# The first two groups of a two-stage kernel run pair by pair, with loads issued in order of need and the first output stage on its own

## The chip, the core and the metric

The kernel runs on one core of one Trainium2 chip. The metric is the device time of one execution in microseconds (us), lower is better. The span of a profile is about 1.7 us shorter than the time of the same execution. Executions are sorted into fast and slow ones (slow: over 1.5% above the fastest of the same kernel); only fast ones are compared below unless the text says otherwise. In the views PE is TensorE (matmuls), PEld its weight loads, DVE VectorE, ACT ScalarE, POOL GpSimd and SP SyncE, which only issues transfers here. A *bank* is the piece of accumulator memory into which TensorE writes a result; an *eviction* is the copy out of it.

## The reference, cut to what matters

```python
for t in range(S):                       # per batch and head, gamma depends on the head
    state = gamma * state + outer(k[t], v[t])
    y[t] = scale * q[t] @ state
x = y, with heads joined                 # 3072 tokens x 512
h = x @ w_in                             # 512 -> 2048
out = (h * cos(h)) @ w_out               # 2048 -> 512
```

The kernel does the recurrence in chunks of 128 steps. One chunk of two batches is a *pair* (12 pairs); two pairs make a *group* of 512 token columns (6 groups). A pair is: conversion of q, k, v to bf16, stage T (transposes of q and k), stage A (scores), masks, stage Y (output into `xt`, and the state). A group then has 16 *F units* (x @ w_in for 128 features, then Sin and a multiply) and 16 *O units* (@ w_out).

## The kernel before

The loads of a pair are shared out between SP's queue and GpSimd's queue, and everything that GpSimd issues or converts stands in one program order:

```python
def load_pair(p):
    for t, src, engs in ((qf, q, (nc.sync, nc.sync)),
                         (kf, k, (nc.gpsimd, nc.gpsimd)),
                         (vf, v, (nc.sync, nc.gpsimd))):    # v of batch 0: SP
        for b in range(2): engs[b].dma_start(...)           # 256 KB each

def unit_f(g, f):                       # needs all 512 columns: both pairs of the group
    for i in range(KIN):
        nc.tensor.matmul(bank, lhsT=w_in_sb[:, i, ts(f, 128)], rhs=xt[g % 2][:, i, :], ...)
    cb = cosb[f % 3]
    nc.scalar.activation(out=cb, in_=bank, func=AF.Sin, bias=halfpi)
    nc.vector.tensor_tensor(out=gt[g % 2][:, f, :], in0=bank, in1=cb, op=ALU.mult)

# start (cut): pairs 0 and 1 without any F; GpSimd issues w_in, pairs 2 and 3, w_out, pair 4
for g in range(NG + 1):
    for s in range(16):
        hf, r = divmod(s, 8);  p = 2 * (g + 1) + hf
        if g < NG: unit_f(g, s)
        if g > 0:  unit_o(g - 1, *divmod(s, 4))
        if p < NP:
            if r == 0:   conv(p)            # q and v on GpSimd, k on VectorE
            elif r == 1: stage_t(p, False)
            elif r == 2: todo = stage_a(p); stage_m(p, todo[0])
            elif r == 3: stage_m(p, todo[1])
            elif r == 6: stage_y(p); ...    # and load_pair(p + 3)
```

## Time and profile before

| | before |
|---|---|
| time, median of 3 executions before the prediction (of 4 in the result) | 242.61 us (241.5) |
| span of the profiled execution | 239.4 us |
| first F unit, first O unit | 23.4 us, 57.8 us |
| first F unit of group 2 | 94.2 us |

This is the page's view of the span in 40 slices of 6 us. A digit is the busy share in tenths, PEclk is the granted TensorE clock. The row counts the time before the first clock record as full, which it was not: in this trace the record begins at about 26 us, and the F units at 23.36 and 25.02 us still take 0.42 us per 128x512 matmul, twice the later 0.216.

```profile
PE   0475409989699999999999999999999999999993
POOL 8907989259999706406024041000000000000000
PEclk9999956999889999999999999999999999999998
DMA  6999999999859354553071061101100111001212
```

From the twelfth slice on TensorE is full; nearly everything that is lost is lost before 66 us. There the DMA row is full and TensorE has holes. TensorE's waits (line, what it waited for, total, times, longest):

```profile
PE bank_67 L167 <- POOL qs_114 L145: 8.8, 1, 8.8
PE bank_69 L167 <- DVE qs_113 L145: 2.8, 1, 2.8
PE bank_63 L216 <- DVE am_1_1_131 L197: 2.2, 1, 2.2
PE bank_65 L167 <- DVE ks_116 L158: 1.2, 1, 1.2
```

The longest, 8.8 us, is for pair 2's q as converted by GpSimd. Busy time by stretch (stretch and its length, then the busy time of PE, PEld, DVE, ACT and POOL, granted clock, DMA share, GB/s); the last row is a group in the steady part:

```profile
25.20:37.00 11.80, 3.01 (x20) 1.71 (x18) 2.14 (x4) 1.93 (x3) 11.07 (x13) 0.68 1.16 267
57.00:93.60 36.60, 34.60 (x271) 17.03 (x270) 21.76 (x32) 18.79 (x28) 26.94 (x29) 0.95 0.71 189
93.60:127.00 33.40, 33.40 (x276) 17.01 (x275) 19.72 (x32) 19.51 (x29) 11.56 (x13) 1.00 0.39 103
```

TensorE works 3.0 of 11.8 us from 25 to 37 us while GpSimd (the fifth number) is busy for 11.1. A steady group takes 33.4 us. The chain of work that ended last (start, length, what) says what GpSimd was busy with:

```profile
6.34 13.21 DMA vf_0_100<-in_v_dram
19.63 2.04 POOL vs_119 L150 x2
23.31 6.85 DMA kf_1_93<-in_k_dram
34.24 1.09 POOL qs_114 L145
60.48 2.86 DVE ks_116 L158 x2
```

One tile, pair 1's v of batch 0 on SP's queue, took 13.2 us to land; GpSimd stood waiting for it, issued the rest of w_in and the loads of pairs 2, 3, w_out and pair 4 after it, and only then converted pair 2's q.

### The profile page before, as it was taken

How to read it: one execution, taken by the hardware profiler on the slowest of the kernel's cores; microseconds unless marked ns; L12 is line 12 of the kernel's file. 1: busy time of each engine (PE TensorE's matmuls, PEld its weight loads, DVE VectorE, ACT ScalarE, POOL GpSimd, SP SyncE). 2: the span in 40 equal slices, each digit the busy share in tenths (PEclk: the TensorE clock that was granted, in tenths of full speed). 3: DMA queues.
4: the chain of work that ended last, by engine and by line, in shares of the span. 5: the costliest groups of instructions: out<-in, count | busy, mean ns of one | idle time of the engine just before them, and what ended most of it. 6: DMA issues, size and time to landing. Idle time of an engine off the chain costs nothing.

```text
span 239.4 us, 4178 instructions
## 1 busy us (share of the span) xinstructions
PE 210.8 (88%) x1664; PEld 108.1 (45%) x1664; DVE 122.0 (51%) x203; ACT 118.8 (50%) x174; POOL 84.0 (35%) x96
## 2 busy tenths in 40 slices
PE   0475409989699999999999999999999999999993
PEld 0264105545345545545555455455455454444441
DVE  4565213968674473466556654753855624343100
ACT  2542305776435655556645646556465564544210
POOL 8907989259999706406024041000000000000000
PEclk9999956999889999999999999999999999999998
DMA  6999999999859354553071061101100111001212
GB/s 164 328 201 222 272 261 196 253 276 297 215 164 267 101 164 98 154 151 92 0 178 44 21 157 45 48 1 47 44 31 16 44 47 44 6 38 44 90 44 88
DMA packets 48020, 29.63 MB, mean 124 GB/s; under 512 B 38529, under 2 KB 42625, under 8 KB 48001
## 3 DMA queue, kind: packets, MB, share of 16 engines
q1 hardware_dynamic: 40896, 15.73, 25.7%
q0 software_dynamic: 7104, 13.63, 22.9%
q8 instruction: 13, 0.21, 0.3%
q14 instruction: 7, 0.05, 0.1%
HBM read 27.26 MB, written 6.29 MB: 140 GB/s over the span
## 4 chain that ended last, share of the span: by engine, by line
PE 74%; DMA 8%; DVE 7%; POOL 3%; issue 2%; SPq 2%; ACT 1%; DVEq 0%; ACTq 0%
PE bank_66 L254 14%; PE bank_63 L254 7%; PE bank_69 L240 6%; PE bank_65 L240 6%; DMA vf_0_100<-in_v_dram 6%; PE bank_64 L240 5%; PE bank_67 L240 5%; PE bank_68 L240 5%; PE bank_67 L254 4%; PE bank_63 L240 4%; PE bank_69 L254 3%; PE bank_68 L254 3%; DMA kf_1_93<-in_k_dram 3%; DVE gt_136 L244 3%; SPq L107 2%
## 5 line engine op out<-in xcount | busy, mean ns | idle before, releaser
L240 PEld LDWEIGHTS <-w_in_sb 128*128 128x128 bf16 x384 | 36.1, 99 | 41.4 <-issue 3.0
L254 PEld LDWEIGHTS <-gt_136 128*128 128x128 bf16 x192 | 19.0, 99 | 23.3 <-issue 1.1
L254 PEld LDWEIGHTS <-gt_137 128*128 128x128 bf16 x192 | 18.8, 98 | 22.7
L254 PE MATMUL bank_66<-w_out_sb,gt_136 128*128 128x512 bf16 x96 | 24.6, 379 | 0.0
L243 ACT ACTIVATE cosb_138<-bank_65,halfpi 128x512 bf16<-128x512 f32 x14 | 9.6, 687 | 15.9 <-PE bank_65 L240 15.9
L254 PE MATMUL bank_63<-w_out_sb,gt_136 128*128 128x512 bf16 x64 | 17.3, 395 | 0.0
L254 PE MATMUL bank_66<-w_out_sb,gt_137 128*128 128x512 bf16 x64 | 16.4, 379 | 0.0
L240 PE MATMUL bank_69<-xt_135,w_in_sb 128*128 128x512 bf16 x44 | 12.1, 402 | 0.0
L254 PE MATMUL bank_67<-w_out_sb,gt_137 128*128 128x512 bf16 x48 | 11.8, 380 | 0.0
L243 ACT ACTIVATE cosb_140<-bank_64,halfpi 128x512 bf16<-128x512 f32 x9 | 6.2, 687 | 9.7 <-PE bank_64 L240 9.7
L240 PE MATMUL bank_63<-xt_134,w_in_sb 128*128 128x512 bf16 x40 | 10.3, 380 | 0.0
L233 DVE CAST stb_133<-st_ps 64x512 bf16<-64x512 f32 x12 | 8.3, 688 | 3.3 <-PE st_ps L228 3.1
L240 PE MATMUL bank_65<-xt_134,w_in_sb 128*128 128x512 bf16 x32 | 9.1, 411 | 0.3 <-ACT xt_134 L220 0.3
L240 PE MATMUL bank_64<-xt_135,w_in_sb 128*128 128x512 bf16 x36 | 9.3, 380 | 0.0
L240 PE MATMUL bank_65<-xt_135,w_in_sb 128*128 128x512 bf16 x36 | 9.3, 380 | 0.0
L240 PE MATMUL bank_67<-xt_135,w_in_sb 128*128 128x512 bf16 x36 | 9.3, 380 | 0.0
L167 PE MATMUL bank_67<-ident,qs_114 128*128 128x128 bf16 x8 | 1.0, 263 | 8.8 <-POOL qs_114 L145 8.8
L240 PE MATMUL bank_68<-xt_134,w_in_sb 128*128 128x512 bf16 x32 | 8.2, 380 | 0.0
L240 PE MATMUL bank_64<-xt_134,w_in_sb 128*128 128x512 bf16 x32 | 8.2, 380 | 0.0
L240 PE MATMUL bank_68<-xt_135,w_in_sb 128*128 128x512 bf16 x32 | 8.2, 379 | 0.0
L254 PE MATMUL bank_68<-w_out_sb,gt_136 128*128 128x512 bf16 x32 | 8.2, 379 | 0.0
L254 PE MATMUL bank_69<-w_out_sb,gt_137 128*128 128x512 bf16 x32 | 8.2, 380 | 0.0
(361 smaller groups left out, 474.5 us busy)
## 6 DMA issues: line engine op xcount, KB each, us to landing
w_in_sb<-in_moe_w_in_dram POOLq DMA_DIRECT2D x4, 512.0 KB, 8.7
w_out_sb<-in_moe_w_out_dram POOLq DMA_DIRECT2D x4, 512.0 KB, 12.6
out_dram<-ob_108 SPq DMA_DIRECT2D x6, 256.0 KB, 2.1
out_dram<-ob_109 SPq DMA_DIRECT2D x6, 256.0 KB, 2.0
out_dram<-ob_110 SPq DMA_DIRECT2D x6, 256.0 KB, 2.0
out_dram<-ob_111 SPq DMA_DIRECT2D x6, 256.0 KB, 2.0
qf_0_78<-in_q_dram SPq DMA_DIRECT2D x3, 256.0 KB, 4.1
qf_1_79<-in_q_dram SPq DMA_DIRECT2D x3, 256.0 KB, 4.7
```

What stands on the lines that cost most here:

```text
L107: engs[b].dma_start(out=t[p % PRE][b], in_=src[2 * bp + b, :, ds(c * C, C)].rearrange("h t d -> t h d"))
L167: nc.tensor.transpose(tr[:, w, a, :], src[:, b, 2 * a : 2 * a + 2, :], ident)
L233: nc.vector.tensor_copy(out=stb[(p + 1) % 2][ts(j, 64), :, :, ts(j, 64)], in_=st_ps[ts(j, 64)])
L240: nc.tensor.matmul(bank, lhsT=w_in_sb[:, i, ts(f, 128)], rhs=xt[g % 2][:, i, :], start=(i == 0), stop=(i == KIN - 1))
L243: nc.scalar.activation(out=cb, in_=bank, func=AF.Sin, bias=halfpi)
L244: nc.vector.tensor_tensor(out=gt[g % 2][:, f, :], in0=bank, in1=cb, op=ALU.mult)
L254: nc.tensor.matmul(bank, lhsT=gt[g % 2][:, f, ts(j, 128)], rhs=w_out_sb[:, f, :], start=(f == 0), stop=(f == KOUT - 1))
```

## The change

The intent: let F start as soon as one pair is there, have F of group 1 to do while the data of pairs 2 and 3 come, and issue loads in the order in which they are needed. The core of the diff (cut):

```diff
-    def load_pair(p): ...
+    def load(eng, p, names): ...              # any tile on any queue
+    def pair_f(p, r):                         # F on the 256 columns of one pair
+        g, hf = divmod(p, 2)
+        for f in (4 * r, 4 * r + 2):
+            bank = banks.take()
+            for e in range(2):                # two f tiles to a bank
+                for i in range(KIN):
+                    nc.tensor.matmul(bank[:, ts(e, 256)], lhsT=w_in_sb[:, i, ts(f + e, 128)],
+                                     rhs=xt[g % 2][:, i, ts(hf, 256)], ...)
+            act(bank, gt[g % 2][:, f : f + 2, ts(hf, 256)])
...
+    load(nc.gpsimd, 1, ("k0", "k1", "v0", "v1"))     # v0 of pairs 1 to 3 no longer on SP
+    load_w_in(0); load_w_in(1)
+    for p in (2, 3): load(nc.sync, p, ("q0", "q1"))
+    load(nc.sync, 4, ("q0", "q1", "v0"))
+    conv_v(0, nc.gpsimd); conv_v(1, nc.gpsimd)
+    load(nc.gpsimd, 2, ("k0", "k1", "v0", "v1"))
+    load_w_in(2); load_w_in(3)
+    load(nc.gpsimd, 3, ("k0", "k1", "v0", "v1"))
+    conv_v(2, nc.gpsimd)
+    for r in range(4): load_w_out(r)
+    load(nc.gpsimd, 4, ("k0", "k1", "v1"))
...
+    stage_t(1, True);  pair_f(0, 0);  m1 = stage_a(1); masks(1, m1);  pair_f(0, 1)
+    stage_y(1, nc.scalar.copy)
+    conv_q(2, nc.vector); conv_k(2, True)            # were GpSimd and VectorE
+    pair_f(1, 0); pair_f(1, 1);  stage_t(2, False);  pair_f(0, 2);  ...   # to pair_f(3, 3)
-    for g in range(NG + 1):
+    for g in range(1, NG + 1):                       # g == 1: O(0) with pairs 4, 5, no F
-            if g < NG: unit_f(g, s)
+            if 1 < g < NG: unit_f(g, s)
```

The semicolons join lines of the original. In the loop a pair's conversions also move from its own first slot to the fifth slot of the pair before.

More of the change, by code (lines that the diff above doesn't have):

```diff
@@ L98, with load @@
     gk = sb([128, NC, H], FP32, "gk")
-    def load_pair(p):
+    SRC = {"q": (qf, q), "k": (kf, k), "v": (vf, v)}
+    def load(eng, p, names):
         bp, c = divmod(p, NC)
-        for t, src, engs in ((qf, q, (nc.sync, nc.sync)),
-                             (kf, k, (nc.gpsimd, nc.gpsimd)),
-                             (vf, v, (nc.sync, nc.gpsimd))):
-            for b in range(2):
-                engs[b].dma_start(
-                    out=t[p % PRE][b],
-                    in_=src[2 * bp + b, :, ds(c * C, C)].rearrange("h t d -> t h d"))
+        for n in names:
+            t, src = SRC[n[0]]
+            b = int(n[1])
+            eng.dma_start(
+                out=t[p % PRE][b],
+                in_=src[2 * bp + b, :, ds(c * C, C)].rearrange("h t d -> t h d"))
     def load_w_in(r):
@@ L123 @@
                    allow_small_or_imprecise_dtypes=True)
-    load_pair(0)
+    load(nc.sync, 0, ("q0", "q1", "v0"))
+    load(nc.sync, 1, ("q0", "q1"))
+    load(nc.gpsimd, 0, ("k0", "k1", "v1"))
     make_identity(nc, ident)
@@ L200, in stage_m, with stage_y @@
             banks.give(bk[j])
-    def stage_y(p):
+    def stage_y(p, copy_st=nc.vector.tensor_copy):
         c = p % NC
@@ L232, in stage_y, with act @@
         for j in range(2):
-            nc.vector.tensor_copy(out=stb[(p + 1) % 2][ts(j, 64), :, :, ts(j, 64)],
-                                  in_=st_ps[ts(j, 64)])
+            copy_st(out=stb[(p + 1) % 2][ts(j, 64), :, :, ts(j, 64)], in_=st_ps[ts(j, 64)])
+    f_no = [0]
+    def act(bank, out):
+        cb = cosb[f_no[0] % 3]
+        f_no[0] += 1
+        nc.scalar.activation(out=cb, in_=bank, func=AF.Sin, bias=halfpi)
+        if len(out.shape) == 3:
+            cb = cb.rearrange("p (f t) -> p f t", f=2)
+            bank = bank.rearrange("p (f t) -> p f t", f=2)
+        nc.vector.tensor_tensor(out=out, in0=bank, in1=cb, op=ALU.mult)
     def unit_f(g, f):
@@ L241, in unit_f @@
                              start=(i == 0), stop=(i == KIN - 1))
-        cb = cosb[f % 3]
-        nc.scalar.activation(out=cb, in_=bank, func=AF.Sin, bias=halfpi)
-        nc.vector.tensor_tensor(out=gt[g % 2][:, f, :], in0=bank, in1=cb, op=ALU.mult)
+        act(bank, gt[g % 2][:, f, :])
         banks.give(bank)
+    def pair_f(p, r):
[5 more added lines that the diff above has]
+                    nc.tensor.matmul(bank[:, ts(e, 256)], lhsT=w_in_sb[:, i, ts(f + e, 128)],
+                                     rhs=xt[g % 2][:, i, ts(hf, 256)],
+                                     start=(i == 0 and e == 0), stop=(i == KIN - 1),
+                                     skip_group_check=True)
+            act(bank, gt[g % 2][:, f : f + 2, ts(hf, 256)])
+            banks.give(bank)
     o_bank = {}
@@ L261, in unit_o, with masks @@
             nc.sync.dma_start(out=out[ds((2 * bp + j % 2) * S + c * C, C), :], in_=o)
-    load_pair(1)
+    load(nc.gpsimd, 1, ("k0", "k1", "v0", "v1"))
     load_w_in(0)
+    load_w_in(1)
+    for p in (2, 3):
+        load(nc.sync, p, ("q0", "q1"))
+    load(nc.sync, 4, ("q0", "q1", "v0"))
+    conv_v(0, nc.gpsimd)
+    conv_v(1, nc.gpsimd)
+    load(nc.gpsimd, 2, ("k0", "k1", "v0", "v1"))
+    load_w_in(2)
+    load_w_in(3)
+    load(nc.gpsimd, 3, ("k0", "k1", "v0", "v1"))
+    conv_v(2, nc.gpsimd)
+    for r in range(4):
+        load_w_out(r)
+    load(nc.gpsimd, 4, ("k0", "k1", "v1"))
+    def masks(p, items):
+        for it in items:
+            stage_m(p, it)
     conv_q(0, nc.vector)
     conv_k(0, True)
-    conv_v(0, nc.gpsimd)
     stage_t(0, True)
-    load_w_in(1)
-    load_w_in(2)
     m0 = stage_a(0)
-    for it in m0:
-        stage_m(0, it)
+    masks(0, m0)
+    conv_k(1, True)
     conv_q(1, nc.vector)
-    conv_k(1, True)
-    conv_v(1, nc.gpsimd)
-    load_w_in(3)
+    stage_y(0, nc.scalar.copy)
     stage_t(1, True)
-    stage_y(0)
+    pair_f(0, 0)
     m1 = stage_a(1)
-    for it in m1:
-        stage_m(1, it)
-    load_pair(2)
-    load_pair(3)
-    stage_y(1)
-    for r in range(4):
-        load_w_out(r)
-    load_pair(4)
-    def conv(p):
-        conv_q(p, nc.gpsimd)
-        conv_k(p, False)
-        conv_v(p, nc.gpsimd)
+    masks(1, m1)
+    pair_f(0, 1)
+    stage_y(1, nc.scalar.copy)
+    conv_q(2, nc.vector)
+    conv_k(2, True)
+    pair_f(1, 0)
+    pair_f(1, 1)
+    stage_t(2, False)
+    pair_f(0, 2)
+    m2 = stage_a(2)
+    masks(2, m2)
+    pair_f(1, 2)
+    pair_f(0, 3)
+    stage_y(2)
+    pair_f(1, 3)
+    conv_v(3, nc.gpsimd)
+    conv_q(3, nc.gpsimd)
+    load(nc.sync, 5, ("q0", "q1", "v0"))
+    load(nc.gpsimd, 5, ("k0", "k1", "v1"))
+    conv_k(3, False)
+    pair_f(2, 0)
+    pair_f(2, 1)
+    stage_t(3, False)
+    pair_f(2, 2)
+    m3 = stage_a(3)
+    masks(3, m3)
+    pair_f(2, 3)
+    stage_y(3)
+    conv_q(4, nc.vector)
+    conv_k(4, False)
+    conv_v(4, nc.gpsimd)
+    load(nc.sync, 6, ("q0", "q1", "v0"))
+    load(nc.gpsimd, 6, ("k0", "k1", "v1"))
+    for r in range(4):
+        pair_f(3, r)
     todo = []
-    for g in range(NG + 1):
+    for g in range(1, NG + 1):
         for s in range(16):
@@ L300 @@
             p = 2 * (g + 1) + hf
-            if g < NG:
+            if 1 < g < NG:
                 unit_f(g, s)
-            if g > 0:
-                unit_o(g - 1, *divmod(s, 4))
+            unit_o(g - 1, *divmod(s, 4))
             if p < NP:
-                if r == 0:
-                    conv(p)
-                elif r == 1:
+                if r == 1:
                     stage_t(p, False)
@@ L314 @@
                     stage_m(p, todo[1])
+                elif r == 4 and p + 1 < NP:
+                    conv_q(p + 1, nc.gpsimd)
+                    conv_k(p + 1, False)
+                    conv_v(p + 1, nc.gpsimd)
                 elif r == 6:
@@ L317 @@
                     if p + 3 < NP:
-                        load_pair(p + 3)
+                        load(nc.sync, p + 3, ("q0", "q1", "v0"))
+                        load(nc.gpsimd, p + 3, ("k0", "k1", "v1"))
 _INS = ['q', 'k', 'v', 'moe_w_in', 'moe_w_out']
```

## The prediction

> **What bounds the kernel now.** From 66 us TensorE hardly waits: in 100.9–134.0, 134.0–167.4 and 167.4–201.0 us the busy-time table shows it busy throughout at granted clock 1.00. There an F or O unit (four 128x512 matmuls) takes 0.863 us, and a group of 16 F, 16 O and two pairs 33.4 us, so 2.9 us per pair. An estimate of all TensorE work is 192 x 0.863 + 12 x 2.9 = 200 us; with 4.9 us before the first matmul and 3.9 us after the last, 209 us. The span is 239.4 us: about 30 us are lost, all in the start.
>
> The chain of waits and TensorE's waits show where: 8.8 us for qs_114 (pair 2), which GpSimd converts only at 34.2 us, although its q landed at 24.1 us: it first issues pairs 2 to 4 and w_out. 2.8 + 2.2 us for pair 1's conversions and masks; vf_0_100 lands 13.2 us after its issue. TensorE runs cold to about 39 us: 0.42 us per 128x512 matmul at 25 us against 0.216 later (granted clock 0.50 in 30–36 us), the state which the Trainium skill, "TensorE: Matmul & The Clock Gate", Part 1, describes for an idle array.
>
> DMA is nearly full up to 60 us (about 250 GB/s). SP's queue moves 256-byte packets and starves beside GpSimd's large ones (40,896 packets for 15.7 MB against 7,104 for 13.6 MB); the Trainium skill, "DMA: Bandwidth & Descriptors", Queues, rings and completion order, says that the engines alternate by packet. SP's 8th, 10th and 12th tiles landed at 24, 35 and 50 us.
>
> **What the change does.** No arithmetic is removed. 256 half-length matmuls are added in place of 128 full ones (estimate 0.11 us each), two f tiles to a bank, so Sin and multiply stay 0.69 us per bank. Weight loads should stay hidden: a load plus a 128-column transpose already takes only 0.055 us. F can start on one pair; F of group 1 fills the waits for pairs 2 and 3; pair 2's q conversion moves to VectorE.
>
> Estimate by engine order: w_in quarter 0 lands and F(0) starts about 17 us (before: 23.4); TensorE is nearly solid from 27 us; pair 2 transposes at 31 us (before: 35.4); pair 3's q (SP's ninth tile) lands about 30–35 us and is converted by 40 us. F of both groups and pairs 0–3 end at about 62 us. Then O(0) alone with pairs 4 and 5: 13.8 + 5.8 us plus about 3 us of new waits, since one 0.86-us unit separates transposes from stage A while two 1.0-us evictions lie between. Group 2 begins at 84.5 us, before at 100.9: 16.4 us earlier. The rest is unchanged.
>
> **Prediction: 226 us, 8 in 10 between 220 and 233.** Faster by over 2%: 0.94; within 2%: 0.05; slower: 0.01.
>
> **Right or wrong will show in:** the first F matmul near 17 us; full clock from about 25 us with 128x256 matmuls 0.11 us apart; no wait over 3 us after 27 us; O(0) from 62 us with waits on qkt evictions; group 2 at 84 us; 33.4 us per group after it.
>
> **What would make it wrong:** N=256 matmuls limited by weight loads (over 0.13 us: +5 us or more); SP's q tiles of pairs 2 and 3 later than 24 and 35 us; multiplies ahead of pair 2's masks stalling TensorE until it goes cold; or fewer stalls than I count, giving 215–220 us.

## The result

The changed kernel took 225.78 us (median of 4 fast executions, 225.59 to 225.99) against 241.5 us (239.88 to 242.84). The ratio is 0.9352, 95% interval 0.9279 to 0.9425. Here and below a ratio is the mean time of one kernel's fast runs over that of the other's of the same rounds, so not quite the ratio of the medians.

| | before | after |
|---|---|---|
| first F unit | 23.4 us | 16.8 us |
| first O unit | 57.8 us, F(1) still to do | 58.0 us, F(1) done |
| first F unit of group 2 | 94.2 us | 78.5 us |
| from there to the end of the span | 145.2 us | 145.4 us |

The whole gain stands at the beginning of group 2 (94.2 - 78.5 = 15.7 us); after it the two kernels take the same time. The slices of the page (now 5.6 us each; the clock record begins just before 20 us):

```profile
PE   1479899989999999999999999999999999999992
POOL 7989848603999957190520610000000000000000
PEclk9999999999999999999999999999999999999999
DMA  6999999999949793925511511011011011110221
```

TensorE is nearly full from the fourth slice. The DMA row is as full as before until some 55 us: no data were saved. All of TensorE's waits that come to half a microsecond or more in the waits by line are in pair 0; the fourth line is one of the longest of the rest:

```profile
PE bank_63 L170 <- POOL ident masks.py:199: 4.9, 1, 4.9
PE bank_63 L170 <- ACT ks_115 L159: 1.8, 1, 1.8
PE bank_64 L170 <- ACT ks_115 L159: 0.5, 1, 0.5
PE bank_69 L265 <- ACT xt_134 L223: 0.4, 1, 0.4
```

The 8.8 us for GpSimd are gone. By stretch, in the columns as above, the third row being the O(0) stage:

```profile
25.20:37.00 11.80, 11.76 (x160) 10.20 (x159) 9.90 (x14) 9.97 (x16) 8.29 (x11) 1.00 1.17 238
37.00:51.00 14.00, 12.74 (x166) 10.60 (x161) 12.51 (x22) 10.87 (x17) 5.84 (x6) 1.00 1.17 244
58.00:78.60 20.60, 19.84 (x211) 10.85 (x209) 12.29 (x16) 8.45 (x13) 20.55 (x22) 1.00 0.79 223
78.60:112.00 33.40, 33.40 (x276) 17.00 (x275) 19.43 (x32) 19.40 (x29) 17.03 (x18) 1.00 0.61 163
```

From 25.2 to 37 us TensorE now works 11.76 us instead of 3.01; it loses 1.26 of 14 us in the next stretch and 0.76 of 20.6 in the O(0) stage, and the group after that takes the same 33.4 us as before. The pieces of the chain that answer to those of before:

```profile
4.51 10.03 DMA qf_1_81<-in_q_dram
14.56 1.20 DVE qs_113 L148
16.85 1.85 PE bank_66 L265 x8
26.27 0.87 PE bank_63 L265 x8
60.37 1.94 ACT qkt_122 L174 x2
```

A tile on SP's queue still leads the chain at the start, but it is pair 1's q, and it landed at 14.5 us. Two banks of F later the clock is full: eight 128x256 matmuls take 1.85 us cold at 16.85 us (where the PEclk row has no record yet) and 0.87 us at 26.27 us. The last piece is new: in the O(0) stage TensorE waits for ScalarE's evictions of the transposes.

### The profile page after: what moved, and what is told of

The parts are those of the page before. It is cut to its first block, busy times and chain, and to the rows that moved or that the text cites. A ratio compares the mean times of both kernels' runs of the same rounds, so it can differ in the third digit from the quotient of the medians.

```text
span 223.9 us, 4434 instructions
## 1 busy us (share of the span) xinstructions
PE 207.6 (93%) x1792; PEld 118.7 (53%) x1792; DVE 124.4 (56%) x201; ACT 121.2 (54%) x180; POOL 83.4 (37%) x95
## 3 DMA queue, kind: packets, MB, share of 16 engines
q1 hardware_dynamic: 37776, 14.95, 26.1%
## 4 chain that ended last, share of the span: by engine, by line
PE 83%; DMA 4%; ACT 4%; DVE 4%; SPq 2%; issue 1%; DVEq 0%; ACTq 0%
PE bank_64 L279 15%; PE bank_63 L279 6%; PE bank_67 L253 5%; PE bank_69 L253 5%; PE bank_65 L253 5%; PE bank_66 L279 5%; DMA qf_1_81<-in_q_dram 4%; PE bank_68 L279 4%; PE bank_66 L253 4%; PE bank_68 L253 4%; PE bank_63 L253 4%; PE bank_65 L279 3%; PE bank_63 L265 2%; PE bank_69 L265 2%; PE bank_66 L265 2%; PE bank_68 L265 2%
## 5 line engine op out<-in xcount | busy, mean ns | idle before, releaser
L253 PEld LDWEIGHTS <-w_in_sb 128*128 128x128 bf16 x256 | 23.8, 98 | 26.9
L279 PEld LDWEIGHTS <-gt_137 128*128 128x128 bf16 x192 | 18.8, 98 | 22.7
L279 PEld LDWEIGHTS <-gt_136 128*128 128x128 bf16 x192 | 18.3, 98 | 21.4
L265 PEld LDWEIGHTS <-w_in_sb 128*128 128x128 bf16 x256 | 25.2, 100 | 5.1 <-issue 0.8
L279 PE MATMUL bank_64<-w_out_sb,gt_136 128*128 128x512 bf16 x96 | 24.2, 380 | 0.0
L279 PE MATMUL bank_64<-w_out_sb,gt_137 128*128 128x512 bf16 x64 | 16.4, 379 | 0.0
L279 PE MATMUL bank_63<-w_out_sb,gt_136 128*128 128x512 bf16 x48 | 12.3, 379 | 0.0
L279 PE MATMUL bank_66<-w_out_sb,gt_137 128*128 128x512 bf16 x48 | 11.8, 379 | 0.0
L236 DVE CAST stb_133<-st_ps 64x512 bf16<-64x512 f32 x10 | 6.9, 687 | 2.6 <-PE st_ps L231 2.4
L253 PE MATMUL bank_63<-xt_134,w_in_sb 128*128 128x512 bf16 x32 | 8.2, 380 | 0.0
L279 PE MATMUL bank_68<-w_out_sb,gt_137 128*128 128x512 bf16 x32 | 8.2, 379 | 0.0
L279 PE MATMUL bank_65<-w_out_sb,gt_136 128*128 128x512 bf16 x32 | 7.9, 380 | 0.0
L244 ACT ACTIVATE cosb_140<-bank_65,halfpi 128x512 bf16<-128x512 f32 x8 | 5.5, 689 | 4.3 <-PE bank_65 L253 3.3
L244 ACT ACTIVATE cosb_139<-bank_67,halfpi 128x512 bf16<-128x512 f32 x7 | 4.8, 687 | 5.3 <-PE bank_67 L253 4.3
L244 ACT ACTIVATE cosb_138<-bank_69,halfpi 128x512 bf16<-128x512 f32 x7 | 4.9, 693 | 4.6 <-PE bank_69 L253 4.3
L214 PEld LDWEIGHTS <-stb_133 128*64 128x64 bf16 x96 | 5.2, 109 | 3.8 <-issue 3.8
L253 PE MATMUL bank_68<-xt_135,w_in_sb 128*128 128x512 bf16 x28 | 7.2, 379 | 0.0
L244 ACT ACTIVATE cosb_138<-bank_63,halfpi 128x512 bf16<-128x512 f32 x7 | 4.8, 689 | 3.6 <-PE bank_63 L253 2.2
L244 ACT ACTIVATE cosb_140<-bank_67,halfpi 128x512 bf16<-128x512 f32 x6 | 4.1, 691 | 4.5 <-PE bank_67 L253 4.3
L244 ACT ACTIVATE cosb_138<-bank_66,halfpi 128x512 bf16<-128x512 f32 x6 | 4.1, 687 | 4.1 <-PE bank_66 L253 2.4
L253 PE MATMUL bank_65<-xt_134,w_in_sb 128*128 128x512 bf16 x24 | 6.2, 380 | 0.0
L253 PE MATMUL bank_67<-xt_134,w_in_sb 128*128 128x512 bf16 x24 | 6.2, 380 | 0.0
```

What stands on the lines that cost most here:

```text
L214: nc.tensor.matmul(yp[ts(j, 64), a, :], lhsT=stb[p % 2][:, b, a, ts(j, 64)], rhs=qt(n, b, a), start=True, stop=False, skip_group_check=True)
L236: copy_st(out=stb[(p + 1) % 2][ts(j, 64), :, :, ts(j, 64)], in_=st_ps[ts(j, 64)])
L265: nc.tensor.matmul(bank[:, ts(e, 256)], lhsT=w_in_sb[:, i, ts(f + e, 128)], rhs=xt[g % 2][:, i, ts(hf, 256)], start=(i == 0 and e == 0), s ...
L279: nc.tensor.matmul(bank, lhsT=gt[g % 2][:, f, ts(j, 128)], rhs=w_out_sb[:, f, :], start=(f == 0), stop=(f == KOUT - 1))
```

## The experiments

My theory: the change wins by doing F of group 1 (13.8 us of TensorE) in gaps of the start. Rival 1: the order of loads and conversions makes the gain. Rival 2: the gain is an earlier full clock. The changed kernel was not run again in the later rounds, so it is compared through absolute times of fast executions, in part from different chips; the kernel before ran in every round, and spreads more than the changed one (237.7 to 247.4 us with its slow executions; the mean of its fast ones is 241.4 us in the changed kernel's round and 239.3 us in that of a, c, d and b).

| run | fast executions | mean, us | ratio to before |
|---|---|---|---|
| changed kernel | 4 of 4 | 225.8 | 0.9352 |
| a_whole_late | 4 of 4 | 231.0 | 0.9653 |
| c_pair_late | 4 of 4 | 230.9 | 0.9647 |
| d_whole_early | 2 of 4 | 229.2 | 0.9576 |
| b_old_loads | 2 of 4 | 234.5 | 0.9798 |
| b2_v_moved | 4 of 4 | 240.8 | 1.0073 |
| b3_three_v | 4 of 4 | 234.1 | 0.9706 |
| b4_k_act | 4 of 4 | 228.1 | 0.9464 |
| m_before_v | 3 of 4 | 238.4 | 0.9974 |
| x_before_warm | 2 of 4 | 238.8 | 0.9991 |
| g_warm | 5 of 6 | 225.8 | 0.9445 |
| f_spread_o | 6 of 6 | 224.4 | 0.9304 |
| h2_best | 1 of 6 | 222.7 | none |

All kernels gave correct results. h2_best has a single fast execution and no ratio.

### Parts of the F order: a_whole_late, c_pair_late, d_whole_early

All three keep the load and conversion order of the changed kernel. They undo, in turn, both parts of the F order, the early F(1) alone, and the half-width units alone.

```diff
 # a_whole_late: no pair_f; the loop starts at g = 0 with whole units
-    for g in range(1, NG + 1):
+    for g in range(NG + 1):
 # c_pair_late: pair_f for pairs 0 and 1 only; F(1) back in the loop
-            if 1 < g < NG: unit_f(g, s)
+            if g < NG: unit_f(g, s)
 # d_whole_early: F(0) in whole units between the stages of pairs 2 and 3,
 # then F(1) as one block
-    for r in range(4): pair_f(3, r)
+    for f in range(16): unit_f(1, f)
```

> Loads, conversions and evictions ordered as in the changed kernel, but F in whole 512-wide units after both pairs of a group, and F of group 1 beside O of group 0 as before. My theory (the gain is F of group 1, 13.8 us of TensorE work, done in gaps of the start): about 231 us, TensorE idle until pair 3's q is converted near 41 us, then group 1 begins near 50 us (before 56.9). Rival 1 (the order of loads and conversions makes the gain): 226 to 227 us. Rival 2 (an earlier full clock makes it): like the changed kernel wherever the clock is full from 20 us.

> Loads as changed, group 0 pair by pair, but F of group 1 stays beside O of group 0 in whole units. My theory: about 230 us: F(0) starts at 17 us, but then nothing is left to do while pair 3's q comes (wait of 4 to 6 us near 37 to 42 us), so close to run a_whole_late. If half-width units by themselves are the gain: 226.

> Loads as changed, F of both groups in whole 512-wide units, F of group 1 as one block after pair 3, O(0) as a stage of its own. My theory: about 231 to 233 us: F(1) moved ahead but with no gap to fill, plus 1.7 us of new waits in the O(0) stage. If moving F(1) ahead by itself were the gain: 226.

Measured: 231.0, 230.9 and 229.2 us (d's two slow executions: 232.7). a and c are where the theory had put them, d just below its 231 to 233. So the new load and conversion order with the old F order is worth about 8 us (231.0 / 0.9653 = 239.3 us for before in these rounds), and the two parts of the F order together a further 5.2 us (231.0 - 225.8), of which half-width units alone give nothing measurable and early F(1) alone at most 1.8. Rival 1 had put a_whole_late at 226 to 227 us, which was too much; still, the larger part of the gain comes from loads and conversions, as it says, and not from my theory's F(1). Half-width units start F at 16.9 us in c as well, but then TensorE runs dry while pair 3's data come. By stretch, c_pair_late:

```profile
37.00:41.00 4.00, 1.77 (x29) 1.40 (x22) 3.27 (x5) 0.88 (x2) 4.00 (x5) 0.68 1.22 195
41.00:45.00 4.00, 4.00 (x25) 2.72 (x25) 0.69 (x1) 2.35 (x4) 1.59 (x2) 0.50 1.22 197
```

TensorE works 1.77 of 4 us there, and the clock is halved for it afterwards (6.8 us in the clock record). The changed kernel puts F of pair 2 in this place. Only when F(1) is cut by pair can its first half go there, which is why d, whose F(1) must wait for pair 3, does not get it: its trace has the same hole (1.86 of 4 us), though the clock stayed full there.

### The load order undone: b_old_loads

```diff
-    load(nc.gpsimd, 1, ("k0", "k1", "v0", "v1")) ...
+    load_old(1); load_w_in(0); conv_v(0, nc.gpsimd); load_w_in(1); load_w_in(2)
+    conv_v(1, nc.gpsimd); load_w_in(3); load_old(2); load_old(3)
+    for r in range(4): load_w_out(r)
+    load_old(4); conv_v(2, nc.gpsimd)         # v of batch 0 on SP, as before
```

> The compute order of the changed kernel with the issue order of the loads of before. My theory: about 229 us, a new wait of some 3 us for pair 2's k (landed at 28.6 and 30.2 us before) on ScalarE. Rival 1 (loads): 237 us or more, most of the gain lost. Rival 2 (clock): 226 to 230.

Measured: 234.5 us fast, and two slow executions at 240.0 and 242.0. My 229 was wrong; this lay closer to rival 1. With a_whole_late it makes a table of two by two: the new loads, with the moved conversions, save 8.3 us under the old F order (239.3 to 231.0); the new loads alone save 8.7 under the new one (234.5 to 225.8); the new F order saves 4.8 us with the old loads and 5.2 with the new. The two parts nearly add, and the loads are the larger one. (The 234.5 rests on two fast executions, the 225.8 comes from another round.) The chain shows the wait I had expected for pair 2's k (7.6 us from issue to landing, and GpSimd had issued it only at 24.1 us, having waited for v), and two things I had not: ScalarE stood for that k longer than I had counted, and VectorE's casts of k near 60 us:

```profile
6.47 14.80 DMA vf<-in_v_dram
24.14 7.60 DMA kf<-in_k_dram
59.91 5.10 DVE ks L165 x2
```

### One tile moved: b2_v_moved, m_before_v

The first reading was that the v tile of pair 1 on SP's queue did all this, since GpSimd waits for it and all its later issues with it.

```diff
 # b2_v_moved: b_old_loads with       # m_before_v: the kernel before with
-    load_old(1)                       -  (vf, v, (nc.sync, nc.gpsimd))
+    load(nc.sync, 1, ("q0", "q1"))    +  (vf, v, (nc.gpsimd if p == 1 else nc.sync,
+    load(nc.gpsimd, 1,                +           nc.gpsimd))
+         ("k0", "k1", "v0", "v1"))
```

> Run b_old_loads with one tile moved: pair 1's v of batch 0 comes through GpSimd's queue instead of being SP's sixth tile. Theory now: the loss of b_old_loads comes from that tile (it landed at 21.3 us there and GpSimd, waiting for it, issued pair 2's k only at 24 us), so GpSimd is free near 16 us, pair 2's k lands near 24 us, and the time falls from 237.7 to 227 to 231 us. Rival (the whole order of the loads matters, q tiles ahead and w_in late): 234 us or more.

> The kernel before with only that one tile moved to GpSimd's queue. Theory: GpSimd's wait of 7.7 us falls to about 1 us, all that it issues and converts after it comes 5 us earlier (qs_114 at 29 us instead of 34), so 234 to 237 us. Rival: no gain, since the DMA is full until 60 us anyway: 239 to 241.

Measured: 240.8 us, 6 us *more* than b_old_loads (other chip), and 238.4 us, between my two expectations and the same as before within the interval (0.9913 to 1.0034). The reading fell. GpSimd did get free early, but then a tile of 256 KB on SP's queue needed 20.5 us. GpSimd's waits in b2_v_moved, and SP's issue of the tile in question:

```profile
POOL vs L157 <- DMA vf<-in_v_dram: 13.8, 2, 13.7
28.64 6.30 SPq L108 DMA_DIRECT2D vf<-in_v_dram  x1
28.64 20.49 DMA vf<-in_v_dram
```

The wait came back in another place: pair 3's v of batch 0, still on SP, needed 20.5 us from issue to landing and arrived at 49 us, with GpSimd waiting 13.7 us for it. In m_before_v it is pair 3's q:

```profile
18.34 29.22 DMA qf<-in_q_dram
```

### No needed tile at SP's tail, then one cast moved: b3_three_v, b4_k_act

```diff
 # b3_three_v: b_old_loads with v of batch 0 of pairs 1, 2 and 3 on GpSimd's queue
-        load(nc.sync, p, ("v0",))
+        load(nc.gpsimd if 0 < p < 4 else nc.sync, p, ("v0",))
 # b4_k_act: b3_three_v and
-    conv_k(4, False)
+    conv_k(4, True)            # pair 4's k cast by ScalarE, not VectorE
```

> Run b_old_loads with batch 0's v of pairs 1, 2 and 3 on GpSimd's queue (b2_v_moved moved only pair 1's and lost, with pair 3's v landing on SP's queue at 49 us). Revised theory: what costs is a tile that pairs 1 to 3 need and that waits at SP's tail; with none there any more 228 to 231 us, and GpSimd's wait for that v is gone. Rival (the place of w_in and w_out ahead of the tiles of pairs 2 and 3 matters as much): 234 us or more.

> Run b3_three_v (234.2 us) with one edit: pair 4's k is cast by ScalarE instead of VectorE. In b3_three_v VectorE's two casts took 5.5 us together at 57 us, beside GpSimd's own DMA issues and conversions, where the same two casts take 0.75 us elsewhere, and TensorE then waited 4.1 us for the multiplies behind them. If that collision cost it: 229.5 to 231 us, and no wait over 1 us for the multiplies near 60 us. If late loads alone explain b3_three_v: 234.

b3_three_v measured 234.1 us: 6.7 less than b2_v_moved, but only 0.4 less than b_old_loads, outside my 228 to 231 and on the rival's side. Its trace again had the two casts. VectorE and GpSimd in b3_three_v at that time:

```profile
57.13 5.50 DVE L165 CAST ks<-kf 128x512 bf16<-128x512 f32 x2
56.61 1.80 POOL L108 DMA_DIRECT2D kf<-in_k_dram  x2
58.40 0.88 POOL L108 DMA_DIRECT2D vf<-in_v_dram  x1
59.30 2.05 POOL L152 TENSOR_TENSOR qs<-qf,gq 128x512 bf16<-128x512 f32 x2
61.30 2.23 POOL L157 TENSOR_TENSOR vs<-vf,gk 128x512 bf16<-128x512 f32 x2
```

Two casts that take 0.75 us together when GpSimd is idle took 5.5 us beside its issues and conversions, and the multiplies of F stand behind them in VectorE's order. The Trainium skill, "SBUF — State Buffer", Who interferes with whom, says that casts can take a pair of memory ports that VectorE shares with GpSimd, and that the later of the two blocks; this trace agrees as far as durations go. No run moved GpSimd's work away from the casts; that it is what stretched them is read from the traces. With the casts moved to ScalarE the time fell to 228.1 us, 6.0 us less from one line, somewhat more than expected. TensorE's wait for those multiplies and the stretch after it, b3_three_v and then b4_k_act:

```profile
PE bank L269 <- DVE gt L252: 4.2, 2, 4.1
62.10:68.90 6.80, 5.27 (x19) 2.73 (x20) 5.41 (x9) 3.08 (x5) 6.78 (x8) 0.50 0.44 125
```

```profile
PE bank L269 <- DVE gt L252: 0.2, 1, 0.2
62.10:68.90 6.80, 6.37 (x71) 3.41 (x71) 4.00 (x6) 2.51 (x3) 6.79 (x8) 1.00 0.60 159
```

The collision therefore costs twice: a wait of 4 us, and then half the clock, which an estimate from the 5.27 us of busy time at 0.50 puts at 2.6 us; together 6.6, near the 6.0 measured.

So of the 8.7 us that undoing the load order costs, moving the three tiles took back 0.4, moving the casts 6.0, and 2.3 us are left (228.1 - 225.8, across chips), near the 3 us for plain lateness of data that I had first written for b_old_loads. In the changed kernel the two casts took 0.42 us each at 53.5 us, while GpSimd stood idle, waiting until 54.05 us for pair 4's v; the same casts in the kernel before are the 2.86 us in its chain. The changed order does not rule the collision out, it escapes it by timing. The kernel before with only those casts moved was not run, so how much of the gain that one line would have brought alone is not known.

### The clock: x_before_warm, g_warm

```diff
+    def dummy(n):              # matmuls on a bank that is free, result unused
+        for _ in range(n):
+            nc.tensor.matmul(banks.free_list[0], lhsT=stb[0][:, 0, 0, :], rhs=..., ...)
 # x_before_warm: before pair 2's transposes in the kernel before
+                if p == 2 and r == 1: dummy(20)
 # g_warm: in the changed kernel, 18 of them in the waits of pairs 0 and 1
```

> The kernel before with 20 idle matmuls on data without use put in TensorE's 8.8-us wait for pair 2's q, so that it is at full clock when the wait ends. My theory: only the few units after the wait get faster, 1.5 to 3 us less than before (237 to 239 us of 240.5). Rival 2 (the clock makes the gain): 233 us or less.

> The changed kernel with 18 idle matmuls in TensorE's waits of the first 16 us. F(0) of pair 0 is cold in the changed kernel (16 matmuls of 0.21 us against 0.109): at full clock 1.6 us less, so 224 to 224.8 us. If the start is set by DMA and evictions alone: 225.5 to 226.

x_before_warm: 238.8 us, ratio 0.9991 (0.9912 to 1.0069), no gain. But the test failed as a test: in its profiled (slow) execution the idle matmuls ended near 30 us, four microseconds too early, and the clock was 0.50 again from 32 to 39 us. It is inconclusive for the clock.

g_warm: 225.8 us in five fast executions, as the changed kernel and outside my 224 to 224.8, so warming the array in the first 16 us bought nothing. Its profile fell in the slow sixth (234.3 us), where TensorE waited 3.8 us for w_in and 4.1 us for multiplies behind a cast of 4.05 us, the collision again; no fast execution was profiled. In the changed kernel quarter 0 of w_in landed 8.2 us after its issue at 8.6 us, at 16.8 us, which is where F starts. That the arrival of w_in sets the pace there is argued from this, not shown.

### More than the change: f_spread_o, h2_best

```diff
 # f_spread_o: stage A and masks of pairs 4 and 5 one O unit later
-                elif r == 2:
+                elif r == (3 if g == 1 else 2):
 # h2_best: that, g_warm's matmuls, and
+    load_w_in(0)                                   # ahead of pair 1's tiles
+    pair_f(0, 0); stage_t(1, True)                 # in this order
+    load(nc.gpsimd, 3, ("k0", "k1", "q0", "q1", "v0", "v1"))
```

> The changed kernel with stage A of pairs 4 and 5 one O unit later in the O(0) stage. The trace shows two waits of 0.87 us for the qkt evictions there: without them 1.7 us less, 224.0 to 224.3 us. If the masks then come too late for stage Y, the wait only moves: 225 to 226.

> A version meant to beat both: quarter 0 of w_in ahead of pair 1's tiles and F(0) of pair 0 ahead of pair 1's transposes, pair 3's q on GpSimd's queue ahead of w_out, idle matmuls in the first waits, and stage A spread as in f_spread_o. By my theory (start set by the order in which data arrive) 220 to 223 us; if the DMA's total rate sets the start whatever the order: 224, as f_spread_o.

f_spread_o: 224.4 us mean (two at 223.5, four at 224.6 to 224.9), 1.4 us under the changed kernel, where 1.7 was expected. TensorE in the changed kernel, where an O unit (0.87 us) starting at 60.61 is followed by half of stage A at 61.57 and by the other half only at 62.35:

```profile
60.61 1.03 PE L279 MATMUL bank_64<-w_out_sb,gt_136 128*128 128x512 bf16 x4
61.57 0.23 PE L191 MATMUL bank_67<-qkt_122 64*128 64x128 bf16 x1
62.35 0.23 PE L191 MATMUL bank_69<-qkt_122 64*128 64x128 bf16 x1 [0.38 <-ACT qkt_122 L174]
```

(the view of waits credits 0.38 us of this to ScalarE; as the next O unit starts at 62.68 and not at 60.61 + 0.87 + 0.55 = 62.03, the pair loses about 0.65 us, not the 0.87 of my expectation), and in f_spread_o, as pieces of its chain, with no gap between O units and stage A:

```profile
61.24 1.73 PE bank L279 x8
62.97 0.55 PE bank L191 x16
```

h2_best gave 222.7 us once and 227.5 to 228.7 us in five slow executions. In the profiled one, pair 1's q took 14.5 us to land (at 18.2 us), w_in now being ahead of GpSimd's tiles. I do not know what its fast execution did differently, and do not count it as better. f_spread_o is the best stable version.

## Why the prediction was right, point by point

The time, 226 against 225.78 us, is closer than its parts were, in part by luck.

- **No arithmetic removed, N=256 at half length, weight loads hidden:** right. Eight 128x256 matmuls take 0.87 us, 0.109 each.
- **First F near 17 us, full clock from about 25 us, no wait over 3 us after 27 us:** right (16.8 us; the clock rises just before 20 us; no single wait after 27 us above 1 us). The Trainium skill, "TensorE: Matmul & The Clock Gate", Part 1, tabulates two clock states, half and full, and adds a third for when three or more cores of a die are busy; here one core runs, and the clock is 0.5 or 1.0 in every record of the kept traces.
- **"F of both groups and pairs 0–3 end at about 62 us":** it was 58.0, 4 us early.
- **"about 3 us of new waits" in the O(0) stage:** in the right place and for the reason given, but two of about 0.65 us. The stage took 20.5 us, not 22.6.
- **"before at 100.9":** wrong. I had taken the fourth F unit of group 2 for its first; in the kernel before it starts at 94.2 us. Both marks were too late, by 6.0 and 6.7 us, so the difference of 16.4 us stood next to a measured 15.7. That the two errors cancel is luck: with 94.2 beside its own 84.5 the prediction would have been 9.7 us of gain, about 233 us, the upper end of its range.
- **SP's starved tiles:** pair 3's second q landed at 40.5 us, later than the 35 that I had named as a danger. It cost nothing, since TensorE reached pair 3's transposes only at 42.3 us, having F of pair 2 to do.
- **What the prediction's reasons missed:** it gave the load order no gain of its own, and my theory before the experiments gave the gain to F(1). a_whole_late shows about 8 us for loads and conversions with the old F order; b_old_loads shows that undoing the loads alone costs as much, while the new F order keeps its 4.8 us; b4_k_act shows that 6 us of such a loss can be two casts meeting GpSimd's work. The F order's 5 us come only with both of its parts.

Left open: the share of the clock in the gain (x_before_warm did not hold the clock up). An estimate from busy times bounds it: the kernel before had TensorE busy for 21 us at half rate (13.3 up to 26.1 us, 4.3 in 29.5 to 39.7, 3.4 in 63.6 to 67.0), the changed one for 10.4 (up to 19.7 us), so a full clock in the difference would be worth at most some 5 us of the 15.7; and the later two stretches begin in or just after waits of TensorE. Open too: how far the loads alone, without the conversions and evictions moved with them, would carry under the old F order. b_old_loads, with two fast executions, suggests nearly all of the 8 us.

## What to carry to other kernels

Filling a wait pays only if there is work small enough to be ready at that moment: half-width units without F(1), or F(1) without half-width units, gave little, and together 5 us. When two queues feed one start, give the queue that gets the smaller share nothing that a waiting engine needs early, and check where the wait goes when one tile is moved, because it can come back larger. Test the parts of a change two by two: here the part that the theory thought small was the larger one. Look at the durations of short casts beside another engine's conversions before calling a delay late data.

## What the Trainium skill lacked or had wrong

- "DMA: Bandwidth & Descriptors", Queues, rings and completion order, says that engines alternate between queues by packet, but not what this does to a queue of small packets beside one of large. Here 256 KB tiles on SP's queue took 13.2 us (before), 20.5 us (b2_v_moved) and 29.2 us (m_before_v) from issue to landing beside GpSimd's stream; the 256 KB output stores late in the kernel before took 2.0.
- "SBUF — State Buffer", Who interferes with whom, lets the later instruction wait until the other has finished, and does not say which goes next when GpSimd has more instructions behind that one. Here a cast of 0.42 us took up to 4.05 us (b3_three_v), longer than any single GpSimd operation beside it (about 1.1 us); that it waited for several in a row is a reading, not shown.
- "TensorE: Matmul & The Clock Gate", Back-to-back issue gap, gives a measured 131 ns per N=512 matmul in a stream with weight loads. Here it is 0.863 / 4 = 216 ns, which is the page's own figure for a matmul alone, and 0.87 / 8 = 109 ns at N=256.
